# Chained integer readings of the softmax in pairs of buffers, a second head group turned on chip in the last unit, and a new planner string

## The chip, the cores and the metric

The kernel runs on one core of one Trainium2 chip. The metric is the device time of one execution in microseconds; the lower, the better. A core has five engines with instruction lists of their own: PE (TensorE, matrix products into PSUM), ACT (ScalarE), DVE (VectorE), POOL (GpSimd) and SP, which here only issues DMAs. They meet through semaphores alone.

## The reference

Two blocks, attention and an MLP, are run twice with the same weights over a sequence of 2048 tokens of 512 values, in bfloat16. Attention has 32 heads of 16 values each.

```python
def _A_ref(x, wqkv, wo):
    B, S, D = x.shape
    H = 32; Dh = D // H
    q, k, v = split_heads(x @ wqkv)                  # each (B, H, S, Dh)
    scores = jnp.einsum("bhqd,bhkd->bhqk", q, k) * Dh ** -0.5
    p = softmax(scores, axis=-1)
    o = jnp.einsum("bhqk,bhkd->bhqd", p, v)
    return merge_heads(o) @ wo

def _B_ref(x, w1, b1, w2, b2):                       # 512 -> 1376 -> 512
    h = gelu_tanh(layernorm(x) @ w1 + b1)
    return h @ w2 + b2

x = A_x
x = x + _A_ref(layernorm(x), A_wqkv, A_wo)
x = x + _B_ref(layernorm(x), B_w1, B_b1, B_w2, B_b2)
x = x + _A_ref(layernorm(x), A_wqkv, A_wo)
x = x + _B_ref(layernorm(x), B_w1, B_b1, B_w2, B_b2)
```

(The two inner functions are shortened; `split_heads` and `merge_heads` stand for the reshapes.) The MLP of the reference normalises its own input once more, which the kernel folds into one normalisation.

## The kernel before

**Work and tiles.** Attention is done for four heads at a time, a head group; there are eight of them. A *unit* is a set of query tokens: 512 of them, in the second attention the last 512 are three units of 256, 128 and 128. A unit and a head group together are a *segment*. A score tile is 128 keys by 512 columns (512 queries, or 4 key blocks by 128 queries in the last units) for one head; there are 4096 of them in the whole kernel. Scores are made by PE (`score`, L1485) from `KT` and `QT`, with the keys on the partitions, into one bank of PSUM for each tile. Layer 1 and layer 3 in the code are the first and the second attention, each with its MLP.

**Two routes from a score to a probability.** ACT takes groups of three and two tiles in turn and writes exp of them to `PT` (L1470). DVE takes single tiles of the key blocks in `DK` by the *integer route*: a score is scaled so that, with a constant added and rounded to an unsigned 16-bit integer, its bits are those of a bfloat16 number near exp. That is the *first reading* (the load, L1570, in `d_load`). A single reading is too coarse, so three more are made from the first by adding 32, 64 and 96 to the integers (`SHIFT`, L1603, in `job_d`); the value matrix is multiplied in advance with a weight for each reading (`vs`, L1236), and PE adds up all four products (L1673). Readings are kept in the buffers `dp`, each of which holds two tiles (a *batch*, `DBATCH = 2`); before the change each of the four readings of a batch takes one of them, one at a time from a pool as it comes to be written. There are 12; numbers 8 to 11 lie where some early q and k rows were kept and join the pool when these are done with.

**The end of a segment.** When all products of a segment are in the accumulator bank, DVE transposes it (L1703), POOL joins the two parts of a unit that is done in two parts, DVE divides (L1729, L1738) into `ob`. When all eight head groups of a unit are in `ob`, four transposing DMAs (`ot_dma`, L1747) write `OT[:, 0:4]`, PE does the output projection (L1752), and then come the residual sum, the normalisation, a transposing DMA to `yT` (L1799), the first MLP product (L1807), bias (L1831), Gelu on ACT (L1846, with a change of ACT's function table there and back) and the second product (L1854). In the last unit (`job_tail`, `tail_tile`) this is shortened: head group 7 is turned on chip by DVE (L1732, L1734) and has its own weight rows in `OT[:, 6]`, so that the DMAs carry only groups 0 to 6; the normalisation (L1932 to L1939) reads PSUM directly.

**What sets the order.** The Python program is a planner. It holds tasks with priorities for every engine, estimates when each could start from durations written beside the instructions, and emits for every engine a fixed list with semaphore waits. Which tiles go by way of DVE is decided there (`take_d`, `d_solo`) from DVE's planned backlog, the free `dp` buffers and the free PSUM banks. Thresholds of these decisions (`Hint.MODES`) are switched every four score groups by one digit of the string `Hint.ORDER`. After planning, `refill` puts matmuls on zeros (L1374, L1376, L1378) into PE's gaps. So every list can change everywhere when the string or a duration does.

The line that makes the second to fourth readings is, before the change, in a loop over three shifts:

```python
for k in range(1, len(SHIFT)):
    v = yield ("get", "dp", sg["i"])
    ... e.tensor_scalar(out=self.dp[:, v, 0:N], in0=self.dp[:, u, 0:N], scalar1=float(SHIFT[k]), scalar2=None, op0=ALU.add)
```

Of the kernel before, what the change touches and what calls it, by code (L numbers as in the profile page):

```python
# [494 lines left out]
DFLY = 4  # L495
DBACK = 2.0
NDP = 12
# [18 lines left out]

class Hint:
# [3 lines left out]
    ORDER = '1030314504013000770002100030001322211720301320152830020099103433349434900224547132333200304108109592073450410120350500000020401300250030190510019545235400070010000400000000003035505051300127003003312013030441301345301551105950944272700400012452100180089448010010094542070017232403400000004593923090885595895934490200'  # L521
# [13 lines left out]
class Builder:  # L535
# [45 lines left out]
    def alloc(self, es):  # L581
# [7 lines left out]
        self.bst = t("bst", [32, 128], BF16)  # L589
# [29 lines left out]
        self.obl = t("obl", [128, 256], BF16)  # L619
# [8 lines left out]
        self.sq0 = t("sq", [128, 1024], BF16)  # L628
        self.n2 = t("n2", [128, 4, 32], F32)
        self.n2k = t("n2k", [128, NT + 1, 32], BF16)  # L630
        self.nm = t("nm", [128, 32], BF16)
        self.qy = t("qy", [128, 4, 32], I32)
        self.qt1 = t("qt1", [128, 4, 32], F32)
        self.qt2 = t("qt2", [128, 4, 32], F32)
        self.q0n = t("q0n", [128, 4, 32], F32)
# [10 lines left out]
        self.gv = self.h16[:, :, :].rearrange("p f n -> p (f n)")  # L646
        self.sbuf_left = nc.sbuf_bytes_remaining
# [12 lines left out]
        pl["dp"] = Pool(range(8))  # L660
# [6 lines left out]
        pl["sq"] = Pool(range(4))  # L667
        pl["n2"] = Pool(range(4))
# [16 lines left out]
    def sqs(self, s):  # L685

        if s == 0:
            return self.sq0[:, :].rearrange("p (h c) -> p h c", c=16)
        return (self.h16[:, 8:10, :] if s == 1 else self.OT[:, 10 - 2 * s:12 - 2 * s, :]).rearrange("p a (h c) -> p (a h) c", c=16)

    def hres(self, fc):

        k = fc // 2
        if k < 4:
            return [("h", k), ("qk", k // 2 + 2, k % 2)]
        return [("h", k), ("sq", 1, 0), ("sq", 1, 1)]
# [89 lines left out]
    def build_startup_late(self):  # L786
# [4 lines left out]
        def fills():  # L791
# [5 lines left out]
            yield f(lambda e: e.memset(self.bst[:, :], 0.0), [("bst",)], 0.3)  # L797
# [11 lines left out]
            yield ("keys", [("oproj", 3, 0)])  # L809
            yield f(lambda e: e.memset(self.OT[:, 6, :], 0.0), [("OT", 6)], 0.5)  # L810
            for hp in range(4):
                yield ld(lambda e, hp=hp: e.dma_start(self.OT[32 * hp:32 * hp + 16, 6, :], wor[7][:, hp, :]), [("OT", 6)], [("wo7", hp)])
# [3 lines left out]
        def bias():  # L816
            yield ("keys", [("wld",)])
            b = yield ("get", "mb")
            yield Task("pe", 3.0, [I(lambda e: e.transpose(self.psbf(b)[:, 0:32], self.bst[:, :], self.ident[0:32, 0:32]), [("bst", 0), ("bst", 1), ("ident",)], [("ps", b)], 0.1)])
# [17 lines left out]
    def flow_weights(self):  # L837
# [5 lines left out]
        def first(fc):  # L843
            M = 128 if fc < nf else self.FLAST
            dst = self.wf[:, fc, 0:4 * M].rearrange("p (c m) -> p c m", m=M)
            return ld(lambda e: e.dma_start(dst, wr1[:, :, fc * 128:fc * 128 + M]), [("wf", fc)], 0.55, 3.0, (2.5, 0.55))
# [7 lines left out]
        yield ("keys", [("kv", 1, tt) for tt in range(self.NT)] + [("wld",)])  # L854
# [70 lines left out]
    def job_qkv_tile(self, L, tt, slot, i, left, prio, what):  # L925
# [77 lines left out]
        SR = [("sq", ss, k) for k in range(k0, k1)]  # L1003
# [20 lines left out]
    def norms(self, dst, res, ss, which, h0=0):  # L1024
# [6 lines left out]
        return I(fn, [("sq", ss, which)], [res], 0.147 + 0.0166 * (32 - h0))  # L1031
# [19 lines left out]
    def job_first_tile(self, tt, slot, i, left, prio):  # L1051
# [14 lines left out]
        ns = yield ("get", "n2")  # L1066
# [7 lines left out]
        def done():  # L1074
            n[0] -= 1
            if n[0] == 0:
                S_.release("n2", ns)
# [26 lines left out]
        def queries():  # L1104
# [11 lines left out]
            yield ("keys", [("qt", 1)])  # L1116
            yield Task("dve", prio + 0.2, [self.norms(self.n2[:, ns, 8:32], ("n2", ns), ss, 0, 8)])
            yield from self.bound_rows(qs, ns, [("n2", ns)], prio - 0.3, "pool", 8)
            done()
# [379 lines left out]
    def take_d(self, hps, lane=None):  # L1499
# [5 lines left out]
        if self.batch is None and (not S_.pools["dp"].free or S_.pools["dp"].waiters or self.flying >= DFLY):  # L1505
            return None
# [33 lines left out]
        if bt is None:  # L1540
            bt = self.batch = {"unit": S_.pools["dp"].free.pop(0), "tiles": [], "loaded": 0, "closed": False}
            self.ptuse[("dp", bt["unit"])] = 1
            self.flying += 1
        w = len(bt["tiles"])
# [21 lines left out]
    def d_load(self, d):  # L1566
# [3 lines left out]
        self.S_.submit(Task("dve", 0.0, [I(lambda e: e.tensor_scalar(out=self.dp[:, u, w * 512:(w + 1) * 512], in0=self.ps[:, b, :], scalar1=BITS0, scalar2=None, op0=ALU.add),  # L1570
# [3 lines left out]
    def d_loaded(self, bt, w, b):  # L1574
# [10 lines left out]
        self.d_ready(bt, 0, bt["unit"], [w])  # L1585
# [4 lines left out]
    def d_ready(self, bt, k, u, ws):  # L1590
        use = ("dp", u)
        self.ptuse[use] = self.ptuse.get(use, 0) + len(ws)
        self.p_ready([bt["tiles"][w] + (("dp", u, w), self.dp[:, u, w * 512:(w + 1) * 512].bitcast(BF16), use, k) for w in ws])

    def job_d(self, bt):
# [4 lines left out]
        for k in range(1, len(SHIFT)):  # L1600
            v = yield ("get", "dp", sg["i"])
            pr = 0.15 if not self.left(sg) and sg is self.segs[self.acc_seg] else 0.5 if self.left(sg) < DURGE else 2.5
            yield Task("dve", pr, [I(lambda e, k=k, v=v: e.tensor_scalar(out=self.dp[:, v, 0:N], in0=self.dp[:, u, 0:N], scalar1=float(SHIFT[k]), scalar2=None, op0=ALU.add),  # L1603
                                     [("dp", u, w) for w in range(n)], [("dp", v, w) for w in range(n)] + self.dres(v), 0.150 + 0.2605e-3 * N, (), "fast")])
            self.d_ready(bt, k, v, range(n))
# [90 lines left out]
    def job_segend(self, sg):  # L1696
# [14 lines left out]
        RO, RD = ("OT", hg), ("den", hg)  # L1711
        if nparts == 2 and part == 0:
            yield Task("dve", 1.2, [I(lambda e: e.tensor_copy(out=self.rowA[:, hg, :], in_=T[:, :, 17]), [RA], [("rowA", hg)], 0.17)])
            if L == 3:
                yield ("keys", [("oproj", 1, self.NC - 1)])
# [328 lines left out]
```

## Time and profile before

| what | value |
|---|---|
| median of 3 runs (lowest, highest) | 1557.55 us (1556.03, 1558.29) |
| the profiled execution: its time, its span | 1557.67 us, 1555.8 us |
| mean granted TensorE clock in it | 0.996 |
| busy: PE, DVE, ACT, POOL | 1480.4, 1479.3, 1513.2, 320.4 us |
| exp groups on ACT (L1470), three and two tiles | 607 and 653 |
| loads on DVE (L1570) | 969 |
| chained readings on DVE (L1603), of two tiles and of one | 1440 and 27 |

The span runs from the first instruction to the last; the time of the execution has another 1.9 us around it. A group line of the profile names line, engine, operation, output and input with their shapes and count; then the busy time of the group and the mean duration in ns of one instruction; then the idle time of the engine in front of the group's instructions, with what ended most of it. Busy time counts overlapping instructions of one engine once, so it may be less than count times mean. A line of the table by stretches has the stretch, its length, busy time and number of instructions of PE, PEld (weight loads), DVE, ACT and POOL, the granted clock, the DMA share and GB/s. A line of a timeline or of the chain has the start and the length of a run of like instructions in us. A line of waits has the total wait, how often, and the longest.

### The profile page before, as it was taken

The page shows a single profiled execution, that of the slowest core. Times are in us where ns is not written, and L with a number is a line of the kernel's source. Part 1 is how long each engine was busy: PE and PEld are TensorE (multiplying, and loading weights), DVE is VectorE, ACT ScalarE, POOL GpSimd, SP SyncE. Part 2 cuts the span into 40 slices and gives each one's busy share as a digit, 9 for nine tenths or more (in the row PEclk, how much of TensorE's full clock was granted, in tenths as well). Part 3 has the DMA queues.
Part 4 walks back from the last instruction along what each step waited for, and adds up shares of the span by engine and source line. Part 5 has one row for each costly group of instructions (what it writes and reads, how often), then busy time and mean ns, then how long its engine had stood idle before and what let it go on. Part 6 is the DMA issues. An engine that isn't in the chain of part 4 may idle for free.

```text
span 1555.8 us, 41772 instructions
## 1 busy us (share of the span) xinstructions
PE 1480.4 (95%) x17565; PEld 492.0 (32%) x17698; DVE 1479.3 (95%) x3319; ACT 1513.2 (97%) x1350; POOL 320.4 (21%) x569
## 2 busy tenths in 40 slices
PE   8989999999999999999999999999999999999998
PEld 3222222232222222232222222222222223345564
DVE  8899999999999999999999899999999999999894
ACT  8999999999999999999999999999999999999995
POOL 3676321002210021103222137210001000010100
PEclk9999999999999999999999999999999999999999
DMA  6653112213221222322832332210102000221221
GB/s 166 124 134 86 32 32 35 59 24 79 79 55 44 46 59 71 69 57 73 148 53 62 64 85 56 57 36 15 32 22 40 20 25 18 39 48 32 62 60 28
DMA packets 212364, 90.53 MB, mean 58 GB/s; under 512 B 182187, under 2 KB 207056, under 8 KB 212176
## 3 DMA queue, kind: packets, MB, share of 16 engines
q1 hardware_dynamic: 212176, 87.86, 25.3%
q8 instruction: 138, 2.26, 0.6%
q14 instruction: 50, 0.41, 0.1%
HBM read 36.74 MB, written 19.48 MB: 36 GB/s over the span
## 4 chain that ended last, share of the span: by engine, by line
ACT 37%; DVE 31%; PE 26%; issue 2%; POOL 2%; DMA 1%; SPq 1%; POOLq 0%; DVEq 0%
ACT PT L1470 36%; DVE dp L1570 12%; DVE dp L1603 10%; PE ps L1485 8%; PE ps L1673 8%; PE ps L1854 3%; PE ps L965 2%; PE ps L1807 2%; DVE accT L1703 1%; DVE st L882 1%; PE ps L1374 1%; DVE n L1030 1%; PE ps L1378 1%; DVE h L1831 1%; ACT h L1846 1%
## 5 line engine op out<-in xcount | busy, mean ns | idle before, releaser
L1470 ACT ACTIVATE PT<-ps 128x1536 bf16<-128x1536 f32 (+1 forms) x1260 | 1429.6, 1294 | 22.5 <-PE ps L1485 19.4
L1570 DVE TENSOR_SCALAR dp<-ps 128x512 uint16<-128x512 f32 x969 | 645.4, 678 | 24.3 <-PE ps L1485 21.4
L1485 PE MATMUL ps<-QT,KT 32*128 32x512 bf16 (+2 forms) x5120 | 603.1, 340 | 27.3 <-DVE dp L1570 8.8
L1603 DVE TENSOR_SCALAR dp<-dp 128x1024 uint16<-128x1024 uint16 (+1 forms) x1467 | 570.1, 429 | 4.8 <-PE ps L1673 2.5
L1673 PE MATMUL ps<-PT,V 128*17 128x512 bf16 (+2 forms) x3899 | 479.4, 339 | 0.0
L1673 PE MATMUL ps<-dp,vs 128*17 128x512 bf16 (+2 forms) x3663 | 456.6, 338 | 1.0 <-DVE dp L1603 0.8
L1485 PEld LDWEIGHTS ps<-QT,KT 32*128 32x128 bf16 x5120 | 173.1, 91 | 541.3 <-ACT PT L1470 274.4
L1211 POOL TENSOR_SCALAR QT<-qraw,scl,qbias 128x512 bf16<-128x512 bf16 (+2 forms) x91 | 71.8, 790 | 794.8 <-PE ps L1485 790.9
L1673 PE MATMUL ps<-dp,V 128*17 128x512 bf16 (+2 forms) x1221 | 221.4, 338 | 2.9 <-DVE accT L1703 2.6
L1673 PEld LDWEIGHTS ps<-dp,vs 128*17 128x17 bf16 x3663 | 122.6, 89 | 122.0 <-issue 92.2
L1378 PE MATMUL ps<-zw 128*32 128x448 bf16 (+20 forms) x1491 | 153.2, 324 | 1.1 <-DVE dp L1570 0.9
L1673 PEld LDWEIGHTS ps<-PT,V 128*17 128x17 bf16 x3899 | 121.5, 89 | 94.0 <-issue 78.8
L1376 PE MATMUL ps<-zw 32*128 32x444 bf16 (+5 forms) x392 | 121.0, 331 | 0.0
L1374 PE MATMUL ps<-zw 128*128 128x448 bf16 (+16 forms) x409 | 98.9, 337 | 5.0 <-DVE dp L1570 2.2
L1807 PE MATMUL ps<-yT,wf 128*128 128x512 bf16 (+4 forms) x401 | 93.1, 336 | 8.3 <-issue 3.2
L965 PE MATMUL ps<-wqkv,xnT 128*128 128x512 bf16 x300 | 87.2, 388 | 9.6 <-issue 4.1
L1236 POOL TENSOR_SCALAR vs<-V 128x340 bf16<-128x340 bf16 (+2 forms) x72 | 61.5, 854 | 30.2 <-PE ps L1673 16.9
L1673 PEld LDWEIGHTS ps<-dp,V 128*17 128x17 bf16 x1221 | 55.1, 89 | 37.5 <-issue 17.1
L1831 DVE TENSOR_SCALAR h<-ps,b1c 128x512 bf16<-128x512 f32 (+3 forms) x99 | 65.3, 665 | 1.2 <-PE ps L1807 0.6
L1703 DVE STREAM_TRANSPOSE accT<-ps 128x512 f32<-128x512 f32 (+2 forms) x96 | 59.0, 614 | 2.6 <-PE ps L1673 2.4
L1378 PEld LDWEIGHTS ps<-zw 128*32 128x32 bf16 x1491 | 52.4, 95 | 24.4 <-DVE dp L1570 6.7
L1374 PEld LDWEIGHTS ps<-zw 128*128 128x128 bf16 x409 | 31.7, 98 | 59.7 <-issue 33.4
(184 smaller groups left out, 876.4 us busy)
## 6 DMA issues: line engine op xcount, KB each, us to landing
vs<-vs_scr SPq DMA_DIRECT2D x64, 255.0 KB, 2.9
wf<-in_B_w_dram SPq DMA_DIRECT2D x90, 128.0 KB, 2.6
q_scr<-qk SPq DMA_DIRECT2D x20, 256.0 KB, 2.0
k_scr<-qk SPq DMA_DIRECT2D x12, 256.0 KB, 2.0
out_dram<-xres SPq DMA_DIRECT2D x16, 128.0 KB, 1.7
vs_scr<-vs SPq DMA_DIRECT2D x8, 255.0 KB, 2.9
xres<-in_A_x_dram SPq DMA_DIRECT2D x7, 256.0 KB, 6.4
v_scr<-vst SPq DMA_DIRECT2D x12, 136.0 KB, 1.7
```

What stands on the lines that cost most here:

```text
L965: yield Task("pe", prio if c0 == 0 else min(prio, HINT.LIN2), [I(lambda e, c=c: e.matmul(self.ps[:, b, :], lhsT=xnT[:, c, :], rhs=self.wqk ...
L1374: fn = lambda e: e.matmul(self.ps[:, b, 0:w], lhsT=self.zw[:, 0:128], rhs=self.zw[:, 0:w], start=st, stop=st, skip_group_check=True)
L1376: fn = lambda e: e.matmul(self.ps[:, b, 0:w], lhsT=self.zw[32 * p:32 * p + 32, 0:128], rhs=self.zw[32 * p:32 * p + 32, 0:w], start=st, sto ...
L1378: fn = lambda e: e.matmul(self.ps[32 * p:32 * p + 32, b, 0:w], lhsT=self.zw[:, 0:32], rhs=self.zw[:, 0:w], start=st, stop=st, skip_group_c ...
L1470: S_.submit(Task("act", 1e-5 * gi, [I(lambda e, pt=pt, n=n, b0=b0: e.activation(out=self.PT[:, pt:pt + n, :], in_=self.ps[:, b0:b0 + n, :] ...
L1485: return [I(lambda e, kb=kb, i=i: e.matmul(self.ps[:, b, i * W:(i + 1) * W], lhsT=self.KT[32 * hp:32 * hp + 32, hg, kb * 128:(kb + 1) * 12 ...
L1570: self.S_.submit(Task("dve", 0.0, [I(lambda e: e.tensor_scalar(out=self.dp[:, u, w * 512:(w + 1) * 512], in0=self.ps[:, b, :], scalar1=BIT ...
L1603: yield Task("dve", pr, [I(lambda e, k=k, v=v: e.tensor_scalar(out=self.dp[:, v, 0:N], in0=self.dp[:, u, 0:N], scalar1=float(SHIFT[k]), sc ...
L1673: ops.append((nth[j, sh] + 0.1 * i, I(lambda e, hp=hp, v=v, ap=ap[:, i * W:(i + 1) * W], first=first and i == 0, W=W: e.matmul(self.ps[32 ...
L1703: yield Task("dve", 0.3, [I(lambda e: e.transpose(self.accT[:, a, 0:W], self.ps[:, ACCB, 0:W]), [("ps", ACCB)], [RA], 0.17 + 0.535 * W / 5 ...
L1807: yield Task("pe", pr if c0 == 0 else min(pr, HINT.LIN2), [I(lambda e, c=c: e.matmul(self.ps[0:M, b, 0:W], lhsT=self.w1(fc, c), rhs=self.y ...
L1831: S_.submit(Task("dve", pr - 0.7, [I(lambda e, fc=fc, M=M, b=b: e.tensor_scalar(out=hv[0:M, fc * W:(fc + 1) * W], in0=self.ps[0:M, b, 0:W] ...
```

## The change

The first chained instruction still makes the second reading from the first; the second one takes first and second reading together, 2048 elements for a full batch, adds 64 and so makes the third and fourth reading at once. For that, buffers are taken in pairs of neighbours: a batch takes a pair when its first tile is loaded and another pair for the third and fourth reading. `dp` grows to 14 buffers (seven pairs), and rows 4 to 7 of `OT` serve as an eighth pair between the units in which they aren't otherwise needed (`DOT`, `otd`, `dpu`, `dpp`). To make room, some small tensors move into others or are shortened: squares for the norm bounds into `yT` (slot 0) and `wf` (slot 4), `bst` and `q0n` into `h16`; the norm slots `n2`, `qy`, `qt1`, `qt2` go from four to two (`NN2`), and are asked for later. In the last unit head group 6 is turned on chip like group 7 (`obl` is used for one after the other), with weight rows in `OT[:, 4]` and `OT[:, 6]` and the turned groups in `OT[:, 5]` and `OT[:, 7]`; the DMAs carry groups 0 to 5. `Hint.ORDER` is another string. `NEED2 = 0` leaves the condition on free buffers as it was.

```diff
-NDP = 12
+NDP = 14
+NN2 = 2
+NEED2 = 0
+DOT = True
-    ORDER = '10303145040130007700021000300013222117203013201528300200991034333...'
+    ORDER = '50331355850001530021014450130210400000030104040309234305039245049...'
...
-        pl["dp"] = Pool(range(8))
+        pl["dp"] = Pool((0, 2, 4, 6) + tuple(range(12, NDP, 2)))
-        pl["sq"] = Pool(range(4))
-        pl["n2"] = Pool(range(4))
+        pl["sq"] = Pool((1, 2, 3, 4))
+        pl["n2"] = Pool(range(NN2))
...
+    def dpu(self, u):
+        return self.dp[:, u, :] if u < NDP else self.OT[:, 2 * (u - NDP) + 4:2 * (u - NDP) + 6, :].rearrange("p a n -> p (a n)").bitcast(U16)
+    def dpp(self, u):
+        return self.dp[:, u:u + 2, :] if u < NDP else self.OT[:, 4:8, :].rearrange("p a n -> p (a n)").bitcast(U16).rearrange("p (u n) -> p u n", u=2)
...
     def job_d(self, bt):
-        for k in range(1, len(SHIFT)):
-            v = yield ("get", "dp", sg["i"])
-            yield Task("dve", pr, [I(lambda e, k=k, v=v: e.tensor_scalar(out=self.dp[:, v, 0:N], in0=self.dp[:, u, 0:N], scalar1=float(SHIFT[k]), scalar2=None, op0=ALU.add),
...
-            self.d_ready(bt, k, v, range(n))
+        yield Task("dve", prio(), [I(lambda e: e.tensor_scalar(out=self.dpu(u + 1)[:, 0:N], in0=self.dpu(u)[:, 0:N], scalar1=float(SHIFT[1]), scalar2=None, op0=ALU.add),
...
+        self.d_ready(bt, 1, u + 1, u, range(n))
+        v = yield ("get", "dp", sg["i"])
+        yield Task("dve", prio(), [I(lambda e: e.tensor_scalar(out=self.dpp(v)[:, :, 0:N], in0=self.dpp(u)[:, :, 0:N], scalar1=float(SHIFT[2]), scalar2=None, op0=ALU.add),
...
+        for i in (0, 1):
+            self.d_ready(bt, 2 + i, v + i, v, range(n))
...
-        if L == 3 and qc == len(self.units[3]) - 1 and hg == 7:
+        if L == 3 and qc == len(self.units[3]) - 1 and hg >= 6:
+            o = 2 * hg - 7
...
-            yield Task("dve", 1.2, [I(lambda e: e.transpose(self.OT[:, 7, 0:W], self.obl[:, 0:W]), ...
+            yield Task("dve", 1.2, [I(lambda e: e.transpose(self.OT[:, o, 0:W], self.obl[:, 0:W]), ...
...
     def job_tail(self, L, qc):
-        yield ("keys", [("ffn1",) + self.prev(L, qc)] + [("ot", L, qc, hg) for hg in range(7)])
+        yield ("keys", [("ffn1",) + self.prev(L, qc)] + [("ot", L, qc, hg) for hg in range(6)])
         for hp in range(4):
-            yield self.ot_dma(hp, range(7), 4 * n, pr)
+            yield self.ot_dma(hp, range(6), 4 * n, pr)
...
     def tail_tile(self, L, qc, tt, slot, i, left):
-            yield self.oproj_mm(b, i, (h0, h0 + 1), 112, 1.5, True)
-        yield ("keys", [("ot", L, qc, 7)])
-        yield Task("pe", pr, [I(lambda e: e.matmul(self.ps[:, b, :], lhsT=self.OT[:, 7, i * 128:(i + 1) * 128], rhs=self.OT[:, 6, :], ...
+            yield self.oproj_mm(b, i, (h0, h0 + 1), 96, 1.5, True)
+        for hg in (6, 7):
+            w, o = 2 * hg - 8, 2 * hg - 7
+            yield ("keys", [("ot", L, qc, hg)])
+            yield Task("pe", pr, [I(lambda e, w=w, o=o, hg=hg: e.matmul(self.ps[:, b, :], lhsT=self.OT[:, o, i * 128:(i + 1) * 128], rhs=self.OT[:, w, :], ...
```

## The prediction

> **What bounds the kernel now.** I read the busy shares first, then the stages, then the chain, then the engines' own pitch.
>
> ```profile
> PE 1480.4 (95%) x17565; PEld 492.0 (32%) x17698; DVE 1479.3 (95%) x3319; ACT 1513.2 (97%) x1350; POOL 320.4 (21%) x569
> DVE  8899999999999999999999899999999999999894
> ACT  8999999999999999999999999999999999999995
> 350.00:400.00 50.00, 48.66 (x480) 14.32 (x478) 48.85 (x107) 49.98 (x46) 10.41 (x17) 1.00 0.32 77
> 1100.00:1150.00 50.00, 48.36 (x534) 13.86 (x535) 49.46 (x113) 50.00 (x46) 1.58 (x2) 1.00 0.10 28
> 1300.00:1350.00 50.00, 49.21 (x692) 17.17 (x688) 50.00 (x117) 50.00 (x46) 1.37 (x2) 1.00 0.14 26
> ```
>
> The last three lines are from the table by stretches of 50 us (columns PE, PEld, DVE, ACT, POOL). ACT and DVE are both full there, and PE's share includes zero matmuls (L1374 to L1378) that the planner adds into gaps. ACT's idle time is 42.6 us in all: 1555.8 less 1513.2, most of it before 150 us and after 1500 us. Between 150 and 1450 us ACT waits for anything only 26 times:
>
> ```profile
> ACT PT L1470 <- PE ps L1485: 8.9, 25, 0.9
> ACT dw L1723 <- DVE dw L1722: 0.6, 1, 0.6
> ```
>
> So **ACT sets the time**, with DVE as co-bound: a score tile is read either by ACT (L1470) or by DVE (L1570, then L1603), and 4096 tiles must be read. ACT takes 607x3 + 653x2 = 3127, DVE 969.
>
> ```profile
> L1470 ACT ACTIVATE PT<-ps 128x1536 bf16<-128x1536 f32 x607 | 919.0, 1514 | 17.0 <-PE ps L1485 14.9
> L1470 ACT ACTIVATE PT<-ps 128x1024 bf16<-128x1024 f32 x653 | 705.7, 1089 | 5.5 <-PE ps L1485 4.5
> L1603 DVE TENSOR_SCALAR dp<-dp 128x1024 uint16<-128x1024 uint16 x1440 | 564.1, 431 | 4.8 <-PE ps L1673 2.5
> 1260.94 99.77 ACT PT L1470 x89
> 1323.95 2.42 DVE L1603 TENSOR_SCALAR dp<-dp 128x1024 uint16<-128x1024 uint16 x7
> 1327.23 1.27 DVE L1570 TENSOR_SCALAR dp<-ps 128x512 uint16<-128x512 f32 x2
> ```
>
> Instructions of one engine overlap, so means overstate them; what counts is the pitch. ACT: 99.77/89 = 1.121 us; one more tile in a group costs 1514 - 1089 = 425 ns; with 3127/1260 = 2.48 tiles in a group, 1.121 - 2.48x0.425 = 0.067 us remains for each group. DVE, from its timeline: seven chained ones in 2.42 us with 0.41 for the last give (2.42 - 0.41)/6 = 0.335 us; two loads in 1.27 us with 0.68 for the last give 0.60 us (0.59, rounded up).
>
> The third view is the end of the chain of waits, after the last exp (ends 1534.44):
>
> ```profile
> 1535.02 6.14 SPq L1747 DMA_TRANSPOSE OT<-ob  x4
> 1539.94 2.55 PE ps L1854 x11
> 1542.49 0.86 PE ps L1752 x4
> 1543.36 0.23 PE ps L1928
> 1543.61 0.71 DVE st L1932
> 1545.57 0.82 DVE xn L1939
> ```
>
> The four transposing DMAs of head groups 0 to 6 leave only when group 6 is normalised (1534.99), and PE does the unit before's second FFN matmuls (L1854) ahead of the output projection (L1752). Group 7's own operand was ready at 1539.68, yet its statistics start at 1543.61.
>
> **What the Trainium skill says.** "VectorE: DVE Perf Modes", section "The perf-mode tier table", gives tensor_scalar on 2048 16-bit elements in SBUF 693 ns. The trace has only the 1024 form (0.41 us uncontended, mean 431 ns); by that page's "Side-by-side" section (4 elements a cycle, 0.96 GHz) 1024 more elements are 0.267 us, an estimate of 0.68 us, a pitch of 0.60. "SBUF — State Buffer", section "Who interferes with whom", says that such an instruction and a GpSimd one share a port pair, which the one that starts first holds to its end while the other is blocked: the trace agrees in kind (in 920 to 1000 us, with POOL busy, one L1603 took 962 ns against a median of 415). "ScalarE: Activation LUTs", section "What ACT_TABLE_LOAD costs", puts an ACTIVATE at 0.833 ns an element: 427 ns for 512, the trace 425.
>
> **The change part by part.** Counts are from the instruction lists that both kernels emit.
>
> *Chained readings.* Before: 480 pairs with three chained instructions each, 9 single tiles with three short ones. After: 488 pairs with one of 1024 and one of 2048 elements, 7 singles. A pair cost 3x0.335 = 1.005 us and costs 0.335 + 0.60 = 0.935: 0.07 saved, not 0.335, because the element work stays and only one instruction's fixed part goes. Over 480 pairs that is 33.6 us of DVE; 8 more pairs, 2 fewer singles and 14 more loads (983 against 969) take about 8x0.935 + 14x0.60 - 2x0.3 = 15 us of it. DVE ends some 19 us lighter, and no more is given to it. By itself a lighter DVE moves no end while ACT is full; it pays through the next item.
>
> *Tiles off ACT.* ACT's list falls from 607 + 653 groups to 598 of three, 659 of two and one of one: 3113 tiles, 1258 groups. 14x0.425 + 2x0.067 = 5.95 + 0.13 = **6.1 us less on the bound engine**. Gelu, table loads and the 16 small exps (L1723) have unchanged counts. Fourteen tiles more on DVE also mean 42 more value matmuls (14 tiles, three readings extra each); PE had zero matmuls to give up, and their number falls.
>
> *The last unit.* Now DMAs carry groups 0 to 5 and start from group 5's normalising; PE's list has the projection's four matmuls and the two for groups 6 and 7 ahead of the eleven of L1854. If nothing else held it, statistics could start 0.3 us after group 7's operand: 1540.0 in place of 1543.6, a gain of 3.6. The DMAs may hold it: they landed 6.8 us after their start before (fourth issue 1539.5, shortest landing 2.3, from 1534.99). In the new DVE list there stand between group 5's normalising and group 7's operand two short chained ones (0.5), ten bias adds (3.3, from x10 in 3.27), and twice the 1.14 us that group 7 took (1538.54 to 1539.68): 6.1 us. So they land 0.7 late; with four matmuls (0.86) and two (0.46) that is statistics at 1541.7, a gain of 1.9. Any wait of DVE in between lengthens the lead, so I take **2.5 us**, ends 0 and 3.6. L1854's 2.55 us go beside the normalisation (1543.61 to 1546.44 = 2.83): cover of 0.28 us. Without it they cost back up to 2.55. One residual add (0.6) now stands ahead of the last copy of yT, beside PE's transposes (0.41): about 0.2, inside the 2.5.
>
> *Queue work.* The weight rows for groups 6 and 7 are eight small DMAs (four before, 0.42 us each on SP): 1.7 us more, now in the middle of the last units, ahead of a vs and a qraw load. A head group there lasts some 7 us (accT transposes, L1703, at 1501.9, 1508.3, 1515.9 and 1523.1) and qraw has two buffers, so I put zero; without that cover it is 1.7 us once. One more memset is on POOL (21% busy).
>
> *Shared buffers.* Two norm slots for four, squares in yT and wf, bst and q0n in h16: no instruction is longer. New waits: squares of the second layer's tiles wait for yT's readers, norms for a slot, and behind these stand the keys of layer three. The chains run on POOL one after another anyway, at low priority, hidden by attention. Before, ACT lost 4.4 us in 900 to 1000 us, where this matters; I put zero, bounds -2 and +5.
>
> *Other order.* The string changes the planner's thresholds and hence every list. ACT's 9.5 us of waits between 150 and 1450 us are drawn anew: zero, bounds -5 and +8.
>
> Sum: -6.1 - 2.5 = -8.6. The profiled execution took 1557.67 (span 1555.8 and 1.9 around it), 0.12 over the median of 1557.55, which I subtract from: **1549.0 us**, -0.55%. A measurement can tell about 0.2%, 3.1 us.
>
> **Rivals.** *Late loads make it slower.* A load has first claim on DVE but can't interrupt: behind a 2048 instruction it waits up to 0.60 instead of 0.335 us. PE's list is in order, a score for DVE waits for that bank, and ACT's next group stands behind it (PE waited for L1570 in 24 places, 8.8 us). With 488 such instructions, an average of 0.0176 us of new ACT idle each eats the 8.6; at 0.03 it is +14.6, so 1557.6 - 8.6 + 14.6 = 1563.6. Against it: the lists were laid out with the longer duration, and ACT has banks of two groups. *The long form runs at half rate*: its 0.53 us of elements become 1.07, 488x0.53 = 260 us on DVE, over 1700 us. Against: same type, same memory, contiguous pairs. *Freed DVE also shortens ACT's waits*: half of the 9.5 goes, 1544. *The gain is lost in redrawn waits or the tail stays held*: 4 to 8 us back, 1553 to 1557. *The pairing saves nothing at all*, if the fixed part is not overlapped: then DVE needs 19 us more than I think and ACT, with 14 tiles fewer, still waits for it: about 1557.
>
> **How the numbers follow.** As worked 0.58 (own range 1545 to 1553), shorter waits 0.16, gain lost 0.14 (half of it still beyond 0.2%), no saving 0.03, late loads 0.07, half rate 0.02. Faster by over 0.2%: 0.58 + 0.16 + 0.07 = 0.81; within: 0.07 + 0.03 = 0.10; slower: 0.07 + 0.02 = 0.09. The range 1542 to 1557 leaves out the last two, 0.09, and the outer parts of the others, about 0.1.
>
> **What would show it.** Right: about 488 instructions of 2048 elements near 0.68 us; ACT near 1507 us busy with idle near 40; the projection ahead of the unit before's FFN, and some 19 us from the last exp to the end (21.4 before). Wrong: a mean of the long form over 0.8 us; ACT idle over 50 us; longer waits of ACT for L1485 with DVE as the cause; the last projection still waiting for DMAs.

## The result and the profile after

The kernel after takes **1542.24 us** in the median of four runs (1541.57 to 1542.83), beside 1557.92 for the kernel before in the same comparison: a ratio of **0.9901, 95% interval [0.9884, 0.9918]**, 15.7 us less. The profiled execution took 1542.35 us with a span of 1540.5. The forecast was 1549.0, a gain of 8.6 us; the direction held, the size was nearly twice that, and the time lies at the lower edge of the stated range (1542 to 1557).

The busy shares and two rows of slices of the page after, to be laid beside the first fence of the prediction:

```profile
PE 1490.5 (97%) x17581; PEld 489.7 (32%) x17581; DVE 1459.9 (95%) x2857; ACT 1505.1 (98%) x1348; POOL 331.0 (21%) x570
...
DVE  8899999999999899999999898999999999999896
...
ACT  8999999999999999999999999999999999999997
```

ACT's busy time fell by 8.1 us (from 1513.2), its idle time by 7.2 (from 42.6 to 1540.5 - 1505.1 = 35.4; 4.9 of the 7.2 lie after the last exp, 2.3 before it). The prediction had 6 for the first and nearly 3 for the second. DVE has 462 instructions fewer and 19.4 us less to do. Middle stretches of 50 us in the table after (columns PE, PEld, DVE, ACT, POOL):

```profile
350.00:400.00 50.00, 49.21 (x513) 14.58 (x506) 49.81 (x97) 49.99 (x45) 11.52 (x20) 1.00 0.27 65
1100.00:1150.00 50.00, 49.29 (x574) 14.58 (x574) 49.95 (x96) 50.00 (x45) 1.53 (x2) 1.00 0.07 17
```

Both engines are as full as before; DVE does it with 97 instructions where it had 107. So the freed time isn't idle time: the plan has spent it on other tiles. The groups by form after, which answer to the group lines of before:

```profile
L1493 ACT ACTIVATE PT<-ps 128x1536 bf16<-128x1536 f32 x598 | 911.7, 1525 | 14.9 <-PE ps L1508 12.8
L1493 ACT ACTIVATE PT<-ps 128x1024 bf16<-128x1024 f32 x659 | 716.5, 1101 | 4.9 <-PE ps L1508 4.0
L1630 DVE TENSOR_SCALAR dp<-dp 128x2048 uint16<-128x2048 uint16 x397 | 277.7, 704 | 2.8 <-PE ps L1701 0.2
L1630 DVE TENSOR_SCALAR OT<-dp 128x2048 uint16<-128x2048 uint16 x49 | 33.5, 684 | 0.2
L1630 DVE TENSOR_SCALAR dp<-OT 128x2048 uint16<-128x2048 uint16 x42 | 28.7, 684 | 0.2
```

The 397, 49 and 42 are the 488 long instructions; those that read or write the eighth pair, in `OT`, cost no more than the others. Their price is read better from the pitch, in DVE's timeline after:

```profile
1328.90 0.68 DVE L1594 TENSOR_SCALAR dp<-ps 128x512 uint16<-128x512 f32 x1
1329.50 0.42 DVE L1625 TENSOR_SCALAR dp<-dp 128x1024 uint16<-128x1024 uint16 x1
1329.83 0.69 DVE L1630 TENSOR_SCALAR dp<-dp 128x2048 uint16<-128x2048 uint16 x1
1330.43 0.69 DVE L1594 TENSOR_SCALAR dp<-ps 128x512 uint16<-128x512 f32 x1
```

From start to start: load 0.60, short form 0.33, long form 0.60 us, as estimated.

**Where the 15.3 us of span went.** The last exp ends at 1524.02 in place of 1534.44, which is 10.4; from there to the end are 16.5 us in place of 21.4, which is 4.9. The part after the last exp, in the chain of waits after:

```profile
1524.21 1.45 PE ps L1836 x24
1525.66 0.77 PE ps L1701 x44
1526.43 0.32 PE ps L1952
1526.76 0.86 PE ps L1781 x4
1527.62 0.51 PE ps L1959 x2
1528.12 0.02 issue
1528.15 0.71 DVE st L1963
```

The projection (L1781) now follows the last value products (L1701) and the product that adds the residual (L1952), with no second FFN product between. Group 7's operand is ready at 1527.66 (DVE's timeline), and the statistics (L1963) start 0.49 us later; before, that gap was 3.93. So 3.4 of the 4.9 us are the held projection. The rest comes ahead of it: behind the last exp PE has 24 first-FFN matmuls left (L1836) where it had 44 (L1807), and group 7's transposes start 2.5 us after the last exp in place of 4.1. That belongs to the plan's other order.

**The clock in the two executions.** Part of the 15.7 us may not be the change's. The profiled execution of before had a mean granted TensorE clock of 0.996, that of after 1.000. The first line below is the span and clock of before; the second is from a run of the next section whose lists are those of before up to the last unit; the third is a stretch of before in which the clock fell to 0.83 (in the same stretch after had 1.00).

```profile
core 0: 1555.8 us, clock 0.996
core 0: 1553.7 us, clock 0.999
80.00:100.00 20.00, 17.28 (x130) 4.41 (x132) 17.87 (x35) 16.25 (x15) 15.37 (x20) 0.83 0.78 161
```

In this stretch ACT was busy for 16.25 us, in the second execution for 18.47. The 31 executions of the kernel before in the three groups of runs below go from 1553.4 to 1556.2 us at a clock of 1.000 up to 1560.7 at 0.994, about 1 us for each 0.001. The median of the 18 among them at 0.999 or 1.000 is 1555.2 us; all four of after had such a clock. Compared with these the gain is 13.0 us, an estimate, since it goes across groups of runs. Whether the clock made these executions longer or a longer idle time lowered the clock is not shown, nor whether the change has a part in it.

### The profile page after: what moved, and what is told of

It is laid out like the page before. It is cut to its first block, busy times and chain, and to the rows that moved or that the text cites. A ratio compares the mean times of both kernels' runs of the same rounds, so it can differ in the third digit from the quotient of the medians.

```text
span 1540.5 us, 41172 instructions
## 1 busy us (share of the span) xinstructions
PE 1490.5 (97%) x17581; PEld 489.7 (32%) x17581; DVE 1459.9 (95%) x2857; ACT 1505.1 (98%) x1348; POOL 331.0 (21%) x570
## 4 chain that ended last, share of the span: by engine, by line
ACT 47%; DVE 25%; PE 23%; issue 2%; POOL 2%; DMA 1%; SPq 0%; POOLq 0%; DVEq 0%
ACT PT L1493 44%; DVE dp L1594 9%; PE ps L1508 7%; PE ps L1701 6%; DVE dp L1630 4%; PE ps L1883 3%; DVE dp L1625 2%; PE ps L988 2%; ACT h L1875 2%; PE ps L1836 2%; PE ps L1397 1%; DVE accT L1731 1%; DVE n L1053 1%; DVE h L1860 1%; DVE OT L1594 1%
## 5 line engine op out<-in xcount | busy, mean ns | idle before, releaser
L1493 ACT ACTIVATE PT<-ps 128x1536 bf16<-128x1536 f32 (+1 forms) x1258 | 1421.4, 1302 | 19.8 <-PE ps L1508 16.8
L1594 DVE TENSOR_SCALAR dp<-ps 128x512 uint16<-128x512 f32 x899 | 599.2, 682 | 32.6 <-PE ps L1508 29.9
L1508 PE MATMUL ps<-QT,KT 32*128 32x512 bf16 (+2 forms) x5120 | 602.1, 339 | 24.5 <-ACT PT L1493 7.4
L1701 PE MATMUL ps<-PT,V 128*17 128x512 bf16 (+2 forms) x3891 | 478.0, 338 | 0.1
L1701 PE MATMUL ps<-dp,vs 128*17 128x512 bf16 (+2 forms) x3377 | 438.9, 336 | 1.5 <-issue 0.6
L1508 PEld LDWEIGHTS ps<-QT,KT 32*128 32x128 bf16 x5120 | 175.0, 91 | 543.1 <-ACT PT L1493 290.9
L1630 DVE TENSOR_SCALAR dp<-dp 128x2048 uint16<-128x2048 uint16 x404 | 280.5, 699 | 2.9 <-PE ps L1701 0.2
L1701 PE MATMUL ps<-dp,V 128*17 128x512 bf16 (+2 forms) x1135 | 210.8, 337 | 1.3 <-DVE accT L1731 0.7
L1625 DVE TENSOR_SCALAR dp<-dp 128x1024 uint16<-128x1024 uint16 (+1 forms) x453 | 192.7, 436 | 2.3
L1701 PEld LDWEIGHTS ps<-dp,vs 128*17 128x17 bf16 x3377 | 115.7, 89 | 110.5 <-issue 81.0
L1701 PEld LDWEIGHTS ps<-PT,V 128*17 128x17 bf16 x3891 | 122.6, 89 | 87.8 <-issue 71.4
L1401 PE MATMUL ps<-zw 128*32 128x448 bf16 (+21 forms) x1389 | 150.1, 323 | 0.3 <-DVE dp L1594 0.2
L1836 PE MATMUL ps<-yT,wf 128*128 128x512 bf16 (+5 forms) x440 | 101.5, 340 | 2.7 <-DMA yT<-xn 1.4
L1397 PE MATMUL ps<-zw 128*128 128x448 bf16 (+15 forms) x382 | 96.8, 341 | 3.1 <-DVE onec L783 2.1
L1701 PE MATMUL ps<-OT,vs 128*17 128x512 bf16 (+2 forms) x310 | 79.0, 360 | 0.0
L1860 DVE TENSOR_SCALAR h<-ps,b1c 128x512 bf16<-128x512 f32 (+4 forms) x99 | 65.6, 666 | 4.5 <-PE ps L1836 3.9
L1701 PEld LDWEIGHTS ps<-dp,V 128*17 128x17 bf16 x1135 | 52.7, 88 | 34.0 <-issue 17.5
```

Source lines behind the costliest of these rows:

```text
L1397: fn = lambda e: e.matmul(self.ps[:, b, 0:w], lhsT=self.zw[:, 0:128], rhs=self.zw[:, 0:w], start=st, stop=st, skip_group_check=True)
L1401: fn = lambda e: e.matmul(self.ps[32 * p:32 * p + 32, b, 0:w], lhsT=self.zw[:, 0:32], rhs=self.zw[:, 0:w], start=st, stop=st, skip_group_c ...
L1493: S_.submit(Task("act", 1e-5 * gi, [I(lambda e, pt=pt, n=n, b0=b0: e.activation(out=self.PT[:, pt:pt + n, :], in_=self.ps[:, b0:b0 + n, :] ...
L1508: return [I(lambda e, kb=kb, i=i: e.matmul(self.ps[:, b, i * W:(i + 1) * W], lhsT=self.KT[32 * hp:32 * hp + 32, hg, kb * 128:(kb + 1) * 12 ...
L1625: yield Task("dve", prio(), [I(lambda e: e.tensor_scalar(out=self.dpu(u + 1)[:, 0:N], in0=self.dpu(u)[:, 0:N], scalar1=float(SHIFT[1]), sc ...
L1630: yield Task("dve", prio(), [I(lambda e: e.tensor_scalar(out=self.dpp(v)[:, :, 0:N], in0=self.dpp(u)[:, :, 0:N], scalar1=float(SHIFT[2]), ...
```

## The experiments

Three questions: what the last unit's part is worth, whether DVE or ACT sets the time, and how much of the gain is the code's and how much the string's. Line numbers in the first one are up to five higher than in the kernel before. Medians below are beside the kernel before on the same chip (1556.1, 1555.7 and 1556.1 us in the three groups of runs). The kernel after was measured only in the comparison above, beside 1557.92; so differences to it are between groups of runs, and uncertain by some 3.5 us (from the intervals of the two ratios).

### The last unit's part alone, and all but it

On the kernel before, only head group 6 turned on chip, with its weight rows and its product (not shown here); string and everything else as before:

```diff
-        if L == 3 and qc == len(self.units[3]) - 1 and hg == 7:
+        if L == 3 and qc == len(self.units[3]) - 1 and hg >= 6:
...
-            yield self.ot_dma(hp, range(7), 4 * n, pr)
+            yield self.ot_dma(hp, range(6), 4 * n, pr)
```

> The kernel before with the last unit's part of the change alone: head group 6 turned on chip, the DMAs carry groups 0 to 5. All lists are those of before up to the last unit; PE's list still has the unit before's eleven FFN matmuls (L1854) ahead of the output projection. Theory (the tail's gain comes from PE's order, the eleven matmuls leaving the way to the statistics): nothing, within 0.5 us of before, since L1854 ended at 1542.49 there and still does. Rival (the DMAs were the hold, group 5 in place of 6 frees it): about 2 us faster than before.

Measured: 1555.92 us, ratio 1.0 [0.9989, 1.0011]. No gain at all. Its chain of waits:

```profile
1535.89 1.28 ACT h L1849
1537.56 2.55 PE ps L1857 x11
1540.10 0.86 PE ps L1755 x4
```

PE's list still has the eleven second FFN products (here L1857) ahead of the projection (L1755). But that isn't the only hold. SyncE's queue in the timeline of the same kernel:

```profile
1525.95 5.79 SPq L1872 DMA_DIRECT2D out_dram<-xres  x2
1531.79 7.37 SPq L1750 DMA_TRANSPOSE OT<-ob  x4
```

Group 5 was normalised at 1522.29, yet the transposing DMAs leave at 1531.79: two output stores stand ahead of them, and the second of these waits for a residual add (L1859) that ends at 1531.37. The last DMA starts at 1536.5 and lands 4.0 us later, at 1540.5, while the eleven end at 1540.1. By these times either hold alone would have kept the gain away, and my theory, PE's order and not the DMAs, has its number but only half its reason. On the kernel after, the same part undone:

```diff
-            for hg in (6, 7):
+            for hg in (7,):
                 w = 2 * hg - 8
...
-            yield self.ot_dma(hp, range(6), 4 * n, pr)
+            yield self.ot_dma(hp, range(7), 4 * n, pr)
```

> The changed kernel with the last unit's part undone: only group 7 is turned on chip. ACT's list is the same; PE's list has the eleven FFN matmuls ahead of the projection again. Theory: 3 to 4 us slower than the changed kernel (the gap between group 7's operand and its statistics goes from 0.5 back to 3.9 us), so about 1545.7. Rival (the tail's 4.9 us come from the shorter way up to the last accumulator alone): under 1 us slower, about 1542.7.

Measured: 1546.41 us (0.993 [0.9915, 0.9946]), 4.2 more than the kernel after, where 3 to 4 were expected. The same picture in its chain:

```profile
1528.47 2.55 PE ps L1883 x11
1531.02 0.86 PE ps L1781 x4
1531.89 0.23 PE ps L1959
```

From the last exp to the end it needs 19.7 us, against 16.5. The DMAs leave with group 6 at 1522.88 and the last lands at 1530.1 (start 1526.7, 3.4 us to landing); the eleven end at 1531.02. Without the eleven the projection could have started about 0.9 us earlier, with an earlier landing alone nothing would have changed. **By these times the part needs three things at once**: DMAs that start from group 5, no store ahead of them on SyncE's queue, and a PE list with the projection ahead of L1883. The kernel after has all three, and the plan decides two of them.

### One more instruction on DVE, and one more on ACT

The lists of the kernel after are kept; each long form is emitted as two instructions on half of it. That was to add 34 us of DVE work and moves nothing.

```diff
-        I(lambda e: e.tensor_scalar(out=self.dpp(v)[:, :, 0:N], in0=self.dpp(u)[:, :, 0:N], ...
+        I(lambda e: [e.tensor_scalar(out=self.dpu(v + i)[:, 0:N], in0=self.dpu(u + i)[:, 0:N], ...) for i in (0, 1)][1],
```

> The changed kernel with the planner's lists kept as they are, but each chained instruction of 2048 elements emitted as two of 1024. DVE gets 488 x (2 x 0.335 - 0.60) = 34 us more work, nothing else changes. Theory (DVE is bound together with ACT, a fixed list has little slack): 15 to 30 us slower than the changed kernel, about 1564. Rival (ACT alone sets the time, the pairing only matters through the tiles that the planner moves): under 5 us slower, about 1545.

Measured: 1565.02 us (1.0052 [1.0036, 1.0068]), 22.8 more than the kernel after, and slower than the kernel before. DVE's busy time rose by 31.3 us (it has 495 instructions more, since the seven of single tiles are split too). The chain by engine of this kernel:

```profile
DVE 64%; PE 23%; ACT 8%; issue 4%; POOL 1%; DMA 0%; SPq 0%; POOLq 0%; DVEq 0%
```

and of the kernel after:

```profile
ACT 47%; DVE 25%; PE 23%; issue 2%; POOL 2%; DMA 1%; SPq 0%; POOLq 0%; DVEq 0%
```

So with the plan fixed, each microsecond of busy time added on DVE costs 0.73 (22.8/31.3) although ACT has not one exp more. ACT pays in waits for scores, between 150 and 1450 us, here and in the kernel after:

```profile
ACT PT L1493 <- PE ps L1508: 21.5, 57, 2.2
ACT PT L1493 <- PE ps L1508: 12.6, 26, 2.0
```

The other side: each two-tile exp is emitted as two of one tile, 659 instructions more on ACT and the same elements.

```diff
-        I(lambda e, ...: e.activation(out=self.PT[:, pt:pt + n, :], in_=self.ps[:, b0:b0 + n, :], ...
+        I(lambda e, ...: [e.activation(out=self.PT[:, pt + i:pt + j, :], in_=self.ps[:, b0 + i:b0 + j, :], ...) for i, j in (((0, 1), (1, 2)) if n == 2 else ((0, n),))][-1],
```

> The changed kernel with the planner's lists kept as they are, but each exp group of two tiles emitted as two instructions of one tile. ACT gets 659 times the fixed part of a group, 0.067 us by the prediction, 44 us more work, nothing else changes. Theory (ACT sets the time nearly everywhere): 30 to 44 us slower than the changed kernel, about 1580. Rival (ACT has hidden slack, DVE sets the time): under 15 us slower.

Measured: 1569.27 us (1.0077 [1.0062, 1.0093]), 27.0 more than the kernel after, a little under what was expected. ACT's busy time rose by 35.4 us to 1540.5, which is 0.054 us for each added instruction (the prediction had 0.067), and 27.0/35.4 = 0.76 of it reached the end. The chain by engine is now

```profile
ACT 72%; DVE 13%; PE 11%; POOL 2%; issue 2%; DMA 0%; SPq 0%; POOLq 0%; DVEq 0%
```

**Both engines bound this plan, about equally**: with a fixed plan, busy time added on either costs about three quarters of itself (0.6 to 0.9, with the uncertainty of such differences). What work taken away would bring without a new plan is not shown by these two.

### The string apart from the code

`Hint.ORDER` is emptied in both kernels (`ORDER = '0'`: the same thresholds everywhere), and exchanged between them.

```diff
-    ORDER = '503313558500015300210144501302104000000301040403092343050392450495084100...'
+    ORDER = '0'
```

> The kernel before with its string replaced by an empty one, so that the planner uses its base thresholds throughout. ACT's list is 3149 tiles in 1264 groups (3127 in 1260 before). Theory (ACT's list sets the time): 22 x 0.425 + 4 x 0.067 = 9.6 us slower than before, about 1566. Rival (the string's worth lies in fewer waits, not in ACT's list): 20 us slower or more.

> The changed kernel with an empty string too: 3132 tiles in 1256 groups, the projection ahead of the FFN matmuls in the last unit as in the changed kernel. Against the kernel before with an empty string ACT's list is 17 x 0.425 + 8 x 0.067 = 7.8 us shorter and the last unit 4 us. Theory (the code brings the gain, each string about the same on top): about 12 us faster than that one, so some 1554, 1557 or less in any case, and 8 to 12 us slower than the changed kernel. Rival (most of the gain came from the new string): within 5 us of the kernel before with an empty string.

```diff
-    ORDER = '503313558500015300210144501302104000000301040403092343050392450495084100...'
+    ORDER = '10303145040130007700021000300013222117203013201528300200991034333...'
```

> The changed kernel with the string of before: 3128 tiles in 1259 groups. Theory (a string fits only the plan it was made for; with another plan it is as good as none): like the changed kernel with an empty string, 1548 to 1556; by ACT's list alone 15 x 0.425 = 6.4 us slower than the changed kernel, 1548.7. Rival (the new string brings nothing of its own): within 3 us of the changed kernel.

> The kernel before with the new string: 3153 tiles in 1268 groups. Theory: 26 x 0.425 + 8 x 0.067 = 11.6 us slower than before, about 1568. Rival (the new string is better on its own): faster than before.

| string | code before | code after |
|---|---|---|
| none | 1591.40 | 1583.92 |
| of the kernel before | 1555.67 | 1583.87 |
| of the kernel after | 1604.90 | 1542.24 (from the comparison above) |

I had expected 1566 by the list for the code before without a string, 1554 for the code after without one, and 1548 to 1568 for the exchanges; all four lie far outside. Two things held: for the first, the rival that a string's worth lies elsewhere than in ACT's list (20 us slower or more); and for the code after, the theory that the old string is as good as none. A string is worth 36 us in the code before and 42 in the code after, and the other code's string is worth nothing (code after) or harms (13.5 us, code before). Nothing here says how well each string is chosen for its code; part of the difference between 36 and 42 may lie there. Without a string the code after keeps a lead of 7.5 us, where 12 were expected. The lists hardly tell this: the code before without a string has only 22 tiles and 4 groups more on ACT, 9.6 us. Its span is 33.5 us longer, of which 15.8 are ACT's busy time and 17.7 its idle time. ACT's waits for scores over the whole span, without and with its own string:

```profile
ACT PT L1470 <- PE ps L1485: 38.7, 95, 3.1
ACT PT L1470 <- PE ps L1485: 19.4, 46, 1.2
```

### Two more plans for each code

Is 7.5 us what the code is worth, or itself one draw? A string of nothing but ones, and one of nothing but sevens, in both codes (`ORDER = '1' * 316` and `'7' * 316` in the code before, 315 in the code after).

> The kernel before with a string of nothing but ones: 3155 tiles in 1265 groups on ACT, six tiles and one group more than with no string (1591.4 us), which is 2.6 us by the list. Theory 'the list decides': 1594 (1590 to 1598). Rival 'a plan is a draw of waits': outside that by 5 us or more, with ACT's waits for scores away from the 28.7 us that they had without a string between 150 and 1450 us.

> The kernel after with a string of nothing but ones (the same thresholds everywhere, the second set). List on ACT: 3135 tiles in 1258 groups, against 3155 in 1265 of the kernel before with the same string. Theory 'the code carries its gain whatever the plan': 20 tiles x 0.425 + 7 groups x 0.067 = 9.0 us by the list and 4 us by the last unit, so 13 us (9 to 16) faster than the kernel before with ones. Rival 'the plan decides, and a plan is a draw': ACT's waits are drawn anew by several us, and the difference lies outside 9 to 16. Both: 20 to 50 us slower than the kernel after with its own string.

> The kernel before with a string of nothing but sevens: 3147 tiles in 1263 groups on ACT, two tiles and a group fewer than with no string (1591.4 us). Theory 'the list decides': 1590.5 (1586.5 to 1594.5). Rival 'a plan is a draw of waits': outside that by 5 us or more.

> The kernel after with a string of nothing but sevens: 3123 tiles in 1253 groups on ACT against 3147 in 1263 of the kernel before with sevens: 24 x 0.425 + 10 x 0.067 = 10.9 us by the list and 4 by the last unit. Theory 'the code carries its gain whatever the plan': 15 us (11 to 18) faster than before with sevens. Rival 'a plan is a draw': outside that.

Measured: ones 1595.53 before and 1594.78 after; sevens 1594.72 and 1594.57. These are two runs each, with ratios to the kernel before known to about 0.4%, so a difference within a pair is known to 8 or 9 us, and none is seen. The lists gave 9.0 and 10.9 us plus the last unit, and for the code after the rival, that the plan decides and is a draw, is the likelier one, by a narrow margin with ones. The code before came out inside its range with ones (1590 to 1598) and just above it with sevens (1586.5 to 1594.5); the code after stayed behind what its list gives. The spans of the profiled executions of the four pairs, taken apart (us, after less before; "end" is the time after the last exp; ACT's busy time there is 7 us in all eight; the last column has the mean granted clock, before and after):

| string | span | ACT busy | end | ACT idle up to the last exp | clocks |
|---|---|---|---|---|---|
| each its own | -15.3 | -8.1 | -4.9 | -2.3 | 0.996, 1.000 |
| none | -7.8 | -9.5 | -3.2 | +4.9 | 1.000, 0.999 |
| ones | +1.4 | -9.2 | -3.3 | +13.9 | 0.999, 0.996 |
| sevens | +0.2 | -8.6 | -3.4 | +12.2 | 1.000, 0.998 |

Two columns hardly move with the plan: 8 to 9.5 us less on ACT and, but for the own pair's 1.6 us of matmuls, 3.2 to 3.4 us off the end. The idle column is the draw, and it has the clock in it: in the first pair the execution of before had the lower one, in the last two that of after. At 1 us for each 0.001 (an estimate from the runs of the kernel before) the four spans would differ by some 11, 9, 2 and 2 us, all in favour of the code after. ACT's waits over the whole span with ones, first of the code after:

```profile
ACT PT L1493 <- PE ps L1508: 49.7, 83, 6.7
```

and of the code before:

```profile
ACT PT L1470 <- PE ps L1485: 33.0, 79, 2.3
```

The code after waits longer at a time (6.7 us at worst), with DVE busy for 91% of the span, less than the 95% of the kernel after. In both codes with ones the chain is 40% PE and 26% DVE. The longest wait stands at the same place in all three plans of the code after without its own string, 6.2 to 7.1 us ending between 952 and 960 us; ahead of it the chain goes through the last norms of the second layer (L1029, L1053, L1195) to the first scores that need them (L1508). Those are among the tensors whose buffers the change rearranged. But the code before waits up to 5.3 us there with sevens, and no run undid the rearranging alone, so that it makes these waits is not shown.

## Why the prediction was right, and where it was too small

**What held.** The chained readings: 488 long instructions with a median of 686 ns (0.68 estimated; 693 in the Trainium skill, "VectorE: DVE Perf Modes", "The perf-mode tier table", with which this case's trace thus agrees), a pitch of 0.60, DVE 19.4 us lighter (19; its own sum gives 18.3). The tiles off ACT: the list gave 6.1 us, busy time fell by 8.1. No transfer held the end. The residual add ahead of the last yT copy cost 0.10 us (0.2), from the start of the normalisation to the end of the copy. ACT's idle time of 35.4 and 16.5 us from the last exp to the end were both better than the "near 40" and "some 19". One sign of being wrong came in part: between 150 and 1450 us ACT's longest wait for scores grew from 0.9 to 2.0 us. DVE isn't seen as the cause, since PE's waits for DVE's loads fell there from 6.6 to 4.1 us.

**Where the rest of the gain came from.** The sum had 8.6 us, the spans differ by 15.3. ACT's busy time fell by 2.0 more than its list. The end gained 2.4 more: 0.9 because the held projection gave 3.4 and not 2.5, and 1.5 because fewer first-FFN matmuls stood behind the last exp, an effect of order. The last 2.3 are ACT's idle time ahead of the last exp, for which the sum had nothing; by stretches (us):

| stretch | before | after |
|---|---|---|
| 0 to 150 | 11.9 | 9.1 |
| 150 to 1450 | 12.1 | 16.0 |
| 1450 to the last exp | 4.3 | 0.9 |

**The term that was mis-sized is "Other order".** It was worked for the middle alone: 9.5 us of waits drawn anew, zero with bounds -5 and +8. There the waits went to 12.8 us, 3.3 the wrong way and inside the bounds. What came the right way lay in the first and the last stretch and behind the last exp, to which the sum gave nothing for order. Some of that may not be order at all: both outer stretches of before have dips of the clock (0.83 from 80 to 100 us, 0.96 from 1450 to the last exp, 1.00 in both after), and the second execution with the lists of before was 2.1 us shorter. The forecast also took its base, 1557.55 us, from executions of which the profiled one had this lower clock, without asking whether after would have it.

A change of string alone moves this kernel by 36 us and more, so the plan was by far the largest unknown of the sum, and I gave it the smallest working. That it went the good way is in part luck: the new string fits the new code and harms the old one, which the prediction did not work out. The runs don't show that the code alone would have given the forecast 8.6; without a string it gave 7.5, with two others no lead that two runs each could show. Nor does a run separate the pairing of readings from the larger number of buffers that came with it.

**The last unit: right in the end, wrong on the way.** The prediction took 2.5 us between 0 and 3.6. Without the draw of the matmuls behind the last exp it is 3.2 to 3.4 (the four pairs and the undone part agree). The step on the way that failed is "So they land 0.7 late". The four DMAs start at 1518.33, and the last lands at 1526.4 (start 1523.1, 3.3 us to landing), 8.1 us later and not 6.8. But group 7's operand is ready 9.3 us later, not 6.1:

```profile
1521.01 0.35 DVE L1860 TENSOR_SCALAR h<-ps,b1c 128x128 bf16<-128x128 f32 x1 [1.59 <-PE ps L1836]
1523.25 0.35 DVE L1860 TENSOR_SCALAR h<-ps,b1c 128x128 bf16<-128x128 f32 x1 [0.53 <-PE ps L1836]
1524.58 2.04 DVE L1860 TENSOR_SCALAR h<-ps,b1c 128x128 bf16<-128x128 f32 x6 [0.98 <-PE ps L1836]
```

These lines of DVE's timeline after show in brackets the idle time ahead: DVE waits 3.1 us for PE between the bias adds. I had added up instructions and no waits, and had written that a wait would lengthen the lead; it did, and put the operand 1.3 us behind the landing, so no transfer held the projection. That SyncE's queue could hold these DMAs for 9.5 us, as in the first experiment (1522.29 to 1531.79), was not among my steps; after, no store stood in the way.

**A sentence without support: "By itself a lighter DVE moves no end while ACT is full".** Making DVE heavier by 31.3 us of busy time in a fixed plan cost 22.8, so DVE's list does not hide behind ACT's. That a lighter one by itself gains nothing is thereby in doubt, though no run took work off DVE with the lists kept. Two engines that are both full in every stretch of 50 us shown could not be ranked by 2% of idle time here. The forecast came out right in sign all the same, because the plan turned DVE's time into tiles off ACT.

**Rivals.** "Freed DVE shortens ACT's waits" (1544) has the nearest number, but not by its reason: half of the 9.5 us between 150 and 1450 us was to go, and they grew to 12.8 (over the whole span ACT waited for scores 16.8 us in place of 19.4). "Late loads" (slower) didn't come: PE waited for L1594 6.5 us in all after, 8.8 for L1570 before. "The gain is lost in redrawn waits" is what the plans of ones and sevens point to; with the string that the change brings it didn't happen. "Half rate" is refuted by the pitch.

**The shared buffers** were put at zero (-2 to +5). Between 600 and 1000 us, where the second layer's norms fall, ACT is idle for 11.8 us after and 9.1 before, and without a string 23.8 and 18.7; with ones and sevens the code after has 1.4 and 3.9 us more. So it is 1.4 to 5.1 us more in the four pairs, up to the upper bound. Here too the draw is mixed in, since no run undid this part alone.

## What to carry to other kernels

Where a planner with many switches makes the lists, a change of code and a new string are two changes: what the code takes off a bound engine (here 8 to 9.5 us in all four plans) can be worked out from instruction counts to some 2 us, but whether it arrives depends on waits that are drawn anew, and the spread between plans (36 us here) is the honest width of that term. Before ranking two full engines, lengthen each in turn with the lists kept; if both answer, the change pays only if the plan moves work between them. And an earlier transfer is worth nothing while a store stands ahead of it on its queue, or other work ahead of its consumer on that engine's list: what counts is both orders, not the readiness of the data alone. And before a difference of 1% is put down to a change, compare the granted clocks of the two executions.

## What was not expected of the hardware

ACT's busy time isn't a property of its list. With the very same list, 1505.1 us in the kernel after became 1512.8 in the one with split long forms: instructions that follow one another closely overlap, and with 57 waits in place of 26 in the middle part fewer did. The means say the same: an exp of three tiles took 1479 ns in the split kernel and 1525 in the kernel after, one of two tiles 1055 and 1101, so each was shorter while their busy time together was longer. So of two kernels' busy times on a full engine some microseconds are closeness, not work, and the 2 us by which ACT's busy time fell beyond its list in the kernel after may be of that kind; that is argued, not shown. The split DVE forms took 31.3 us more busy time over 495 added instructions, 0.063 us each; an added ACTIVATE took 0.054.
